# A fused attention, expert and gating kernel: decay factors, tile 0 and tile 1 loaded and scored in another order

## The chip, the core and the metric

The kernel runs on one core of a Trainium2 chip. The metric is the device time of one execution in microseconds (us), as the median of several runs. A profiled execution gives the trace that is read here; it records when each instruction of each engine began and ended, and each transfer. The engines are TensorE (PE in the rows, PEld for its loads of weights), VectorE (DVE), ScalarE (ACT), GpSimd (POOL) and SyncE (SP), which issues most of the transfers.

## What is computed

Three layers follow each other. The first is a linear attention with decay over 2 batches of 8 heads, 768 positions and 64 features, in blocks:

```
intra = einsum('bhic,bhjc->bhij', qb, kb) * Dmask      # Dmask: lam ** (i - j) for j <= i, else 0
intra = einsum('bhij,bhjd->bhid', intra, vb)
inter = einsum('bhid,bhde->bhie', qb * lam_pow, kv_state)
out   = intra + inter
kv_state = lam_block * kv_state + einsum('bhsd,bhse->bhde', kb * rev_pow, vb)
```

The second sends each position to one of 8 experts (the choice of the position before may be kept), which is a product with `w1` (512 x 1024), a maximum with zero and a product with `w2` (1024 x 512), weighted with the softmax of the choice. The third is `(sigmoid(conv(x)) * (x @ w_val)) @ w_out` with a convolution over 5 positions.

## The kernel before

The 1536 positions are cut into 12 tiles `g` of 128, six of each batch. In the first stage, up to about 69 us, each tile runs through the same steps. The later stages (experts one after the other, then convolution and projection) are not touched by the change.

The steps of a tile, by the names of the functions in the code:

- `load_qk(g, part)` (lines 82 to 89) has SyncE load the four quarters of a tile, 256 KB each: quarters 0 and 1 hold queries and keys for the scores (half 0 and half 1), quarter 2 the keys by position, quarter 3 the values. Two quarters with one tile buffer go in one load of 512 KB.
- `scores(g, half)` (line 289): TensorE multiplies keys and queries, 4 matmuls for a half, that is 8 passes, 16 for a tile. The result lies in the banks `ps0` and `ps1`.
- `mask(g)` or `mask_half(g, half)` (lines 301 to 313): VectorE multiplies the scores with the decay mask `dm`.
- `queries(g)` (line 265): VectorE multiplies the queries with the powers `lq`. `powers(hps)` (line 121) makes `lq` by scans on VectorE from the decay factors `lam_sb`; `dm` comes from eight scans of the same factors (line 118).
- `keys(g, hs)` (line 276): ScalarE multiplies the keys of some heads with their decay, one instruction a head. `keys_rest(g)` (line 283): VectorE does the last four heads in one instruction.
- `mix_state(g)`, `mix(g, half)` (lines 315 to 334): TensorE adds the part of the state (not for tile 0) and the part of the masked scores into `po`. `mixed(g)` (line 336): ScalarE copies `po` into `xt`.
- `next_state(g)`, `keep_state(g)`, `decay(g)`: the new state, by TensorE into `sp`, by ScalarE (tile 0) or VectorE out of it, and GpSimd or ScalarE for its decay.
- `turned(g, ks)` (line 380): TensorE turns `xt` back to rows and makes the logits, into the two banks `rt` of the pool `ps_1`, of which there is one buffer. `logits`, `choice`, `shift`, `exponents` and `token_rows` read it on VectorE and ScalarE.

The order of the instructions on each engine is written out by hand: in the block from line 545 on, every engine takes its instructions in the order in which the functions are called. TensorE first runs `warm(8)`, eight matmuls on zeros, then the scores of tile 0, `warm(3)`, the mixing of tile 0, the scores of tile 1, and the rest of tile 0 between the steps of tile 1. From tile 3 on a loop does the same for each tile. The decay factors (6 KB) are loaded by ScalarE's queue at line 67; SyncE's queue begins with the four quarters of tile 0 (lines 105 to 108), each by itself, then two loads of 512 KB for each of the tiles 1 and 2.

Of the kernel before, what the change touches and what calls it, by code (L numbers as in the profile page):

```python
# [8 lines left out]
F32 = mybir.dt.float32  # L9
# [10 lines left out]
B, H, S, D = 2, 8, 768, 64  # L20
DM, E, FF = 512, 8, 1024
P = 128
# [4 lines left out]
HP = H // 2  # L27
# [17 lines left out]
def fused_kernel(ctx, tc, qkv, lam, wgl, w1, w2, wv, cw, wo, out, dbg=None):  # L45
    nc = tc.nc
# [14 lines left out]
    def w4(shape, dtype, name):  # L61
        return w4_p.tile(shape, dtype, name=name, tag="w4")
# [1 line left out]


    lam_sb = const.tile([P, H + HP], F32, name="lam_sb")
    nc.scalar.dma_start(lam_sb, lam)

    ps_ms = ExitStack()
    ps_m = ps_ms.enter_context(tc.tile_pool(name="ps_m", bufs=1, space=PSUM, side="right"))  # L70
# [4 lines left out]
    ps_1 = act.enter_context(tc.tile_pool(name="ps_1", bufs=1, space=PSUM))  # L75
# [6 lines left out]
    def load_qk(g, part=slice(0, 4)):  # L82
        for i in range(2):
            a0, a1 = max(part.start, 2 * i), min(part.stop, 2 * i + 2)
            if a0 < a1:
                if (g, i) not in qk_t:
                    qk_t[g, i] = w4([P, 2, 512], F32, f"qk{i}")
                nc.sync.dma_start(qk_t[g, i][:, a0 - 2 * i:a1 - 2 * i, :],
                                  qkv[g].rearrange("p (a n) -> p a n", a=4)[:, a0:a1, :])
# [12 lines left out]
    identr = const.tile([P, P], F32R, name="identr")  # L102
    wgl_sb = const.tile([P, KD, 9], F32, name="wgl_sb")
    with tc.manual_schedule(engines={mybir.EngineType.SP, mybir.EngineType.DVE}):
        load_qk(0, slice(0, 1))
        load_qk(0, slice(1, 2))
        load_qk(0, slice(3, 4))
        load_qk(0, slice(2, 3))
        load_qk(1, slice(0, 2))
        load_qk(1, slice(2, 4))  # L110
        load_qk(2, slice(0, 2))
        load_qk(2, slice(2, 4))
        nc.vector.memset(ones, 1.0)
        nc.vector.tensor_copy(ident16, ident)
        nc.vector.tensor_copy(identr, ident)

        for h in (0, 1, HP, HP + 1, 2, 3, HP + 2, HP + 3):
            nc.vector.tensor_tensor_scan(dm[:, h, :], lam_sb[:, h:h + 1].to_broadcast([P, P]), last_first, 0.0,
                                         op0=MUL, op1=ADD)

    def powers(hps):

        for hp in hps:
            nc.vector.tensor_tensor_scan(lq[:, hp, :], lam_sb[:, H + hp:H + hp + 1].to_broadcast([P, P]), ones, 1.0,
                                         op0=MUL, op1=MUL)
# [62 lines left out]
    def load_next(n=1):  # L188
        for _ in range(min(n, len(w_src))):
            tiles, src = w_src.pop(0)  # L190
            raw = w4([P, 1024], F32, "wraw")
            nc.sync.dma_start(raw, src)
            tiles.append([raw])
# [65 lines left out]
    sm_t, qs_t, kd_t, xt_t, ps_t, po_t, st_t, sd_t = {}, {}, {}, {}, {}, {}, {}, {}  # L259
# [5 lines left out]
    def queries(g):  # L265
        if g % NC > 0:
            qs_t[g] = qs = at_p.tile([P, HP, P], F32, name="qs", tag="qs")
            nc.vector.tensor_tensor(qs.rearrange("p (a h) i -> p a (h i)", a=2), qk_t[g, 0][:, :, 0:256],
                                    lq.rearrange("p (a h) i -> p a (h i)", a=2), op=MUL)

    def key_tile(g):
        if g not in kd_t:
            kd_t[g] = at_p.tile([P, H, D], F32, name="kd", tag="kd")
        return kd_t[g]

    def keys(g, hs=range(HK)):

        if g % NC < NC - 1:
            kd = key_tile(g)
            for h in hs:  # L280
                nc.scalar.activation(kd[:, h, :], qk_t[g, 1][:, 0, h * D:(h + 1) * D], AF.Copy, scale=dm[:, h, P - 1:P])

    def keys_rest(g):
        if g % NC < NC - 1:
            nc.vector.tensor_tensor(
                key_tile(g)[:, HK:H], qk_t[g, 1][:, 0, HK * D:].rearrange("p (h d) -> p h d", h=H - HK),
                dm[:, HK:H, P - 1:P].to_broadcast([P, H - HK, D]), op=MUL)

    def scores(g, half):
        t = qk_t[g, 0]  # L290

        if half == 0:
            ps_t[g] = [ps_s.tile([P, HP, P], F32, name=f"ps{rh}", tag=f"ps{rh}") for rh in range(2)]
        for hp in (2 * half, 2 * half + 1):
            for rh in range(2):
                r = slice(rh * 64, rh * 64 + 64)
                c0 = (hp % 2) * P
                nc.tensor.matmul(ps_t[g][rh][:, hp, :], t[r, half, 256 + c0:256 + c0 + P], t[r, half, c0:c0 + P],  # L298
                                 start=True, stop=True)
# [7 lines left out]
    def mask_half(g, half):  # L307
        if half == 0:
            sm_t[g] = at_p.tile([P, 2, HP, P], F32, name="sm", tag="sm")
        hs = slice(2 * half, 2 * half + 2)  # L310
        for rh in range(2):
            nc.vector.tensor_tensor(sm_t[g][:, rh, hs], ps_t[g][rh][:, hs],
                                    dm[:, rh * HP + 2 * half:rh * HP + 2 * half + 2, :], op=MUL)

    def mix_state(g):

        po_t[g] = ps_1.tile([P, 2, 512], F32, name="po", tag="po")
        if g % NC > 0:
            qs = qs_t.pop(g)
            for hp in range(HP):  # L320
                for hl in range(2):
                    rh = hl ^ hp % 2
                    r = slice(rh * D, (rh + 1) * D)
                    nc.tensor.matmul(po_t[g][hl * D:(hl + 1) * D, hp % 2, hp // 2 * P:(hp // 2 + 1) * P],  # L324
                                     state[g][r, hp, :], qs[r, hp, :], start=(hp < 2), stop=False)

    def mix(g, half):
        c = g % NC
        for hp in (2 * half, 2 * half + 1):
            for hl in range(2):  # L330
                h = (hl ^ hp % 2) * HP + hp
                nc.tensor.matmul(po_t[g][hl * D:(hl + 1) * D, hp % 2, hp // 2 * P:(hp // 2 + 1) * P],  # L332
                                 qk_t[g, 1][:, 1, h * D:(h + 1) * D], sm_t[g][:, h // HP, hp, :],
                                 start=(c == 0), stop=(c == 0 or hp >= HP - 2))

    def mixed(g):
        xt_t[g] = xt = at_p.tile([P, KD, P], F32, name="xt", tag="xt")
        nc.scalar.copy(xt.rearrange("p (j b) n -> p j b n", b=2),
                       po_t.pop(g)[:, :, 0:2 * P].rearrange("p b (j n) -> p j b n", j=2))
# [12 lines left out]
    def bank(g):  # L352
        if g not in sp_t:
            sp_t[g] = ps_1.tile([P, 512], F32, name="sp", tag="sp")
        return sp_t[g]

    def next_state(g):
        if g % NC < NC - 1:
            st_t[g] = st = bank(g)[:, 0:HP * D].rearrange("p (h d) -> p h d", h=HP)
            kd = kd_t.pop(g)  # L360
            for hp in range(HP):
                for rh in range(2):
                    h = rh * HP + hp
                    nc.tensor.matmul(st[rh * D:(rh + 1) * D, hp, :], kd[:, h, :], qk_t[g, 1][:, 1, h * D:(h + 1) * D],  # L364
                                     start=True, stop=True)
# [14 lines left out]
    def turned(g, ks=range(KD)):  # L380
        if 0 in ks:
            rv_t[g] = ps_1.tile([P, 2, 512], F32, name="rt", tag="rt")
        xt, rt = xt_t[g], rv_t[g]
        for k in ks:
            if k < 2:
                nc.tensor.matmul(rt[:, 0, k * P:k * P + XL], xt[:, k, :], wid[:, k, :], start=(k == 0), stop=False,  # L386
                                 skip_group_check=True)
            else:
                nc.tensor.matmul(rt[:, 0, P:XL], xt[:, k, :], wgl_sb[:, k, :], start=False, stop=(k == KD - 1),  # L389
                                 skip_group_check=True)  # L390
                nc.tensor.transpose(rt[:, 1, (k - 2) * P:(k - 1) * P], xt[:, k, :], ident)  # L391
# [153 lines left out]
    with tc.manual_schedule(engines=order_a):  # L545
# [6 lines left out]
        load_qk(3)  # L552
        load_qk(4)
        load_next()
        powers((0, 1))
        mix_state(0)
        mix(0, 0)
        mix(0, 1)
        mixed(0)
        keys_rest(0)  # L560
        keys(0)
        powers((2, 3))
        scores(1, 0)
        scores(1, 1)
        queries(1)
        turned(0, (0, 1))
        mask_half(1, 0)
        mask_half(1, 1)
        next_state(0)
        keep_state(0)  # L570
        turned(0, (2, 3))
        keys(1)
        keys_rest(1)
        decay(1)
# [380 lines left out]
    early, pt0, yg1 = {}, [], {}  # L955
# [424 lines left out]
def build(nc, arrays):  # L1380
    args = [nc.dram_tensor(f"in_{n}_dram", a.shape, mybir.dt.from_np(a.dtype), kind="ExternalInput").ap()
            for n, a in zip(NAMES, arrays)]
    out = nc.dram_tensor("out_0_dram", (TOK, DM), F32, kind="ExternalOutput").ap()
    with tile.TileContext(nc) as tc:
        fused_kernel(tc, *args, out)
# [11 lines left out]
```

## Time and profile before

| | us |
|---|---|
| median of 3 runs | 320.91 (320.7 to 321.35) |
| the profiled execution | 320.72 |
| its span, first to last instruction | 319.0 |
| TensorE busy in the span | 311.5 (98%) |
| VectorE busy | 260.8 (82%) |
| ScalarE busy | 207.2 (65%) |
| GpSimd busy | 89.8 (28%) |

Times in the rows count from the first instruction of the span. Matmuls are pipelined, so the length of one says less than the distance of a group's beginning to that of the next.

### The profile page before, as it was taken

To read this page: it belongs to the slowest core of one execution; us is meant where nothing else is said; L and a number is where in the kernel's file an instruction comes from. 1 tells how busy PE (TensorE), PEld (TensorE's weight loads), DVE (VectorE), ACT (ScalarE), POOL (GpSimd) and SP (SyncE) were. 2 spreads that over 40 slices of the span, in tenths; PEclk is the share of its full clock that TensorE was granted. 3 is DMA by queue.
4 is the path that set the end of the run, shared out by engine and by line. 5 is a ranking of instruction groups with operands and counts; after the bars stand their busy time and mean duration, and the time that the engine had idled before them with its cause. 6 is when DMAs were issued, how large, how long until landed. Compare 5 with 4: busy or idle time off the path is not lost.

```text
span 319.0 us, 7297 instructions
## 1 busy us (share of the span) xinstructions
PE 311.5 (98%) x2707; PEld 275.9 (86%) x2707; DVE 260.8 (82%) x564; ACT 207.2 (65%) x516; POOL 89.8 (28%) x114
## 2 busy tenths in 40 slices
PE   7999999999999999999999999999999999999995
PEld 3888888889889899899798897988987989989984
DVE  6888899888779979869799797797845899977970
ACT  1679899986557666576567665765656676674641
POOL 8000000204454550542525506433334302020000
PEclk9999999999999999999999999999999999999999
DMA  6999898339779699599598698993305402321112
GB/s 207 403 411 395 301 350 304 125 108 369 258 265 362 247 298 374 204 318 355 158 362 326 184 387 339 325 381 115 107 20 130 132 3 90 109 69 67 65 39 103
DMA packets 27543, 73.09 MB, mean 229 GB/s; under 512 B 3814, under 2 KB 8172, under 8 KB 27500
## 3 DMA queue, kind: packets, MB, share of 16 engines
q1 hardware_dynamic: 24756, 65.07, 56.3%
q0 software_dynamic: 2304, 7.42, 7.2%
q8 instruction: 25, 0.41, 0.5%
q14 instruction: 18, 0.15, 0.1%
q10 hardware_dynamic: 440, 0.05, 0.1%
HBM read 57.79 MB, written 14.73 MB: 227 GB/s over the span
## 4 chain that ended last, share of the span: by engine, by line
PE 93%; DVE 3%; DMA 2%; SPq 1%; ACT 0%; issue 0%; ACTq 0%
PE ph L906 27%; PE py L920 19%; PE pv L1065 11%; PE py L1091 10%; PE py L930 6%; PE ps L298 4%; PE po L332 3%; DMA qk<-in_qkv_dram 2%; PE rt L386 2%; PE po L324 2%; PE sp L364 1%; PE px L879 1%; PE rt L389 1%; PE rt L391 1%; PE pt L1019 1%; PE px L525 1%
## 5 line engine op out<-in xcount | busy, mean ns | idle before, releaser
L203 DVE TENSOR_TENSOR wlo<-wraw,whi 128x1024 fp32r<-128x1024 f32 (+1 forms) x69 | 85.6, 1266 | 12.8 <-ACT whi L198 12.8
L906 PE MATMUL ph<-xh,whi 128*128 128x240 f32 x512 | 87.2, 276 | 0.0
L906 PEld LDWEIGHTS ph<-xh,whi 128*128 128x128 f32 x512 | 77.3, 189 | 2.0 <-issue 1.5
L906 PE MATMUL ph<-xh,wlo 128*128 128x240 f32 x256 | 69.9, 274 | 0.0
L198 ACT CAST whi<-wraw 128x1024 fp32r<-128x1024 f32 (+1 forms) x69 | 65.5, 989 | 2.3 <-DVE wlo L203 2.3
L920 PE MATMUL py<-whi,hh 128*128 128x512 f32 x176 | 56.5, 392 | 0.0
L906 PEld LDWEIGHTS ph<-xh,wlo 128*128 128x128 f32 x256 | 48.4, 189 | 0.0
L1051 DVE SCALAR_TENSOR_TENSOR gt<-yt,cw_sb,gt 128x256 f32<-128x256 f32 x96 | 39.0, 477 | 1.1 <-ACT gt L1043 1.1
L920 PEld LDWEIGHTS py<-whi,hh 128*128 128x128 f32 x176 | 33.0, 188 | 6.7
L909 ACT ACTIVATE hh<-ph 128x480 fp32r<-128x480 f32 x32 | 18.3, 572 | 31.5 <-PE ph L906 29.3
L1065 PEld LDWEIGHTS pv<-yh,wv_t 128*128 128x128 f32 x288 | 35.2, 192 | 0.7 <-ACT gt L1043 0.4
L1065 PE MATMUL pv<-yh,wv_t 128*128 128x256 f32 x288 | 35.7, 283 | 0.0
L227 POOL TENSOR_TENSOR f64a<-f64a,f64s 128x512 f32<-128x512 f32 (+1 forms) x9 | 19.7, 2187 | 55.6 <-DVE f64s L226 55.6
L920 PE MATMUL py<-wlo,hh 128*128 128x512 f32 x88 | 34.4, 391 | 0.0
L1091 PE MATMUL py<-wo_t,gh 128*128 128x512 f32 (+1 forms) x156 | 34.1, 376 | 0.0
L1091 PEld LDWEIGHTS py<-wo_t,gh 128*128 128x128 f32 x156 | 27.4, 188 | 5.0
L911 DVE SCALAR_TENSOR_TENSOR hh<-ph,hh 128x480 fp32r<-128x480 f32 x32 | 20.9, 652 | 6.4 <-ACT hf L910 6.4
L859 POOL DMA_INDIRECT xr<-xd,idx x14 | 19.3, 1378 | 7.2 <-DVE cnt L757 4.2
L920 PEld LDWEIGHTS py<-wlo,hh 128*128 128x128 f32 x88 | 16.5, 188 | 3.2
L930 PE MATMUL py<-wraw,hf 128*64 128x256 f32 x160 | 18.4, 382 | 0.0
L298 PE MATMUL ps<-qk 64*128 64x128 f32 x192 | 16.5, 295 | 0.4 <-DMA qk<-in_qkv_dram 0.4
L930 PEld LDWEIGHTS py<-wraw,hf 128*64 128x64 f32 x160 | 11.0, 137 | 5.5
(201 smaller groups left out, 499.1 us busy)
## 6 DMA issues: line engine op xcount, KB each, us to landing
wraw<-in_w_dram SPq DMA_DIRECT2D x64, 512.0 KB, 6.6
qk<-in_qkv_dram SPq DMA_DIRECT2D x22, 512.0 KB, 7.7
ys<-yo SPq DMA_DIRECT2D x16, 256.0 KB, 4.1
xd<-xtok SPq DMA_DIRECT2D x12, 260.0 KB, 3.9
ys<-warm_sb SPq DMA_DIRECT2D x24, 128.0 KB, 1.9
out_dram<-oo SPq DMA_DIRECT2D x11, 256.0 KB, 2.0
wraw<-in_w_val_dram SPq DMA_DIRECT2D x4, 512.0 KB, 4.0
wraw<-in_w_out_dram SPq DMA_DIRECT2D x4, 512.0 KB, 8.8
```

Of the source, the lines that this page charges most:

```text
L198: nc.scalar.copy(w[1][:, cs], w[0][:, cs])
L203: nc.vector.tensor_tensor(w[2][:, cs], w[0][:, cs], w[1][:, cs].bitcast(F32), op=SUB)
L227: nc.gpsimd.tensor_tensor(a.bitcast(F32), a.bitcast(F32), s.bitcast(F32), op=ADD)
L298: nc.tensor.matmul(ps_t[g][rh][:, hp, :], t[r, half, 256 + c0:256 + c0 + P], t[r, half, c0:c0 + P], start=True, stop=True)
L859: nc.gpsimd.indirect_dma_start(xr[:, t, :], None, xd, bass.IndirectOffsetOnAxis(ap=idx[:, 2 * e + t:2 * e + t + 1], axis=0))
L906: nc.tensor.matmul(ph[:, fi, :], w1_t[e][k][1 + a][:, f * P:(f + 1) * P], xh[b][:, k].rearrange("p t n -> p (t n)")[:, 0:C1], start=first, ...
L911: nc.vector.scalar_tensor_tensor(hh[:, 1, :, 0:C1], ph, 0.0, hh[:, 0, :, 0:C1].bitcast(F32), op0=ALU.max, op1=SUB)
L920: nc.tensor.matmul(py, hhs[f // 2][:, a, f % 2, t * P:(t + 1) * P], w2_t[e][f // 2][1 + b][:, (f % 2) * DM:(f % 2 + 1) * DM], start=(n == ...
L930: nc.tensor.matmul(py[i * NW:(i + 1) * NW, 0:DM // 2], hf[:, f, :], w2_t[e][f // 2][0][:, (f % 2) * DM + i * DM // 2:(f % 2) * DM + (i + 1 ...
L1051: nc.vector.scalar_tensor_tensor(gt[:, k, :], yt_t[b, k][:, c0 + j:c0 + j + 256], cw_sb[:, k, j:j + 1], gt[:, k, :], op0=MUL, op1=ADD)
L1065: nc.tensor.matmul(pv[:, mi, :], wv_t[:, a, k * DM + m * P:k * DM + (m + 1) * P], yh[b][:, k, :], start=first, stop=last)
L1091: nc.tensor.matmul(po, gh[a][:, k, t * P:(t + 1) * P], wo_t[:, b, k * DM + cs.start:k * DM + cs.stop], start=(i == 0), stop=(i == 11))
```

## The change

The decay factors are loaded as the first entry of SyncE's queue, not by ScalarE. Tile 0 comes in two loads of 512 KB (first the quarters for the scores, then keys and values) instead of four of 256 KB. The scores of tile 1 are put ahead of the mixing of tile 0; they use the `rt` banks of `ps_1` instead of `ps0` and `ps1`. All eight heads of tile 0's keys go to ScalarE, ahead of the copy of the mixed tile, and VectorE's instruction for the last four heads of tile 0 is gone. VectorE makes the masks of tile 1 right after those of tile 0, then all powers at once, then the queries of tile 1. TensorE makes the state of tile 0 ahead of the whole of tile 0's turning, which is no longer cut in two.

```diff
-    nc.scalar.dma_start(lam_sb, lam)
...
-        load_qk(0, slice(0, 1))
-        load_qk(0, slice(1, 2))
-        load_qk(0, slice(3, 4))
-        load_qk(0, slice(2, 3))
+        nc.sync.dma_start(lam_sb, lam)
+        load_qk(0, slice(0, 2))
+        load_qk(0, slice(2, 4))
         load_qk(1, slice(0, 2))
         load_qk(1, slice(2, 4))
         load_qk(2, slice(0, 2))
...
-    def scores(g, half):
+    def scores(g, half, early=False):
         t = qk_t[g, 0]
 
-        if half == 0:
+        if half == 0 and early:
+            rt = ps_1.tile([P, 2, HP, P], F32, name="rt", tag="rt")
+            ps_t[g] = [rt[:, rh] for rh in range(2)]
+        elif half == 0:
             ps_t[g] = [ps_s.tile([P, HP, P], F32, name=f"ps{rh}", tag=f"ps{rh}") for rh in range(2)]
...
         load_qk(3)
         load_qk(4)
         load_next()
-        powers((0, 1))
+        scores(1, 0, True)
+        scores(1, 1, True)
+        keys(0, range(H))
         mix_state(0)
         mix(0, 0)
         mix(0, 1)
-        mixed(0)
-        keys_rest(0)
-        keys(0)
-        powers((2, 3))
-        scores(1, 0)
-        scores(1, 1)
-        queries(1)
-        turned(0, (0, 1))
         mask_half(1, 0)
         mask_half(1, 1)
+        mixed(0)
+        powers(range(HP))
         next_state(0)
         keep_state(0)
-        turned(0, (2, 3))
+        queries(1)
+        turned(0)
         keys(1)
         keys_rest(1)
         decay(1)
```

## Rows read from the trace of the kernel before

**Rows 1.** Windows: length, busy time by engine, granted clock, DMA share, GB/s.
```profile
13.00:14.00 1.00, 1.00 (x22) 1.00 (x24) 0.83 (x3) 0.94 (x7) 0.00 (x0) 1.00 1.02 418
...
90.00:240.00 150.00, 150.00 (x1096) 134.61 (x1092) 124.86 (x195) 94.38 (x153) 60.32 (x50) 1.00 0.75 269
```

**Rows 2.** Waits of TensorE's matmuls, the largest after 10 us: total, times, longest.
```profile
PE px L525 <- DVE oh L517: 0.5, 1, 0.5
```

**Rows 3.** Chain of waits from 0 to 14.6 us: start, length, what.
```profile
2.68 6.37 DMA qk<-in_qkv_dram
...
9.18 1.16 PE ps L298 x16
...
11.01 0.62 PE sp L364 x16
...
12.39 0.60 PE po L324 x16
12.99 1.02 PE po L332 x16
```

**Rows 4.** Timeline of TensorE's matmuls, 0 to 9 us: start, length, what.
```profile
1.26 3.23 PE L542 MATMUL pidx<-warm_sb 128*128 128x512 f16 x8 [1.26 <-DVE warm_sb L78]
...
5.57 0.82 PE L542 MATMUL pidx<-warm_sb 128*128 128x512 f16 x3
7.21 1.60 PE L332 MATMUL po<-sm,qk 128*64 128x128 f32 x16 [0.82 <-DVE sm L312]
```

**Rows 5.** Timeline of SyncE: the first and second load issued.
```profile
0.81 0.40 SPq L88 DMA_DIRECT2D qk<-in_qkv_dram  x1
...
1.27 0.42 SPq L88 DMA_DIRECT2D qk<-in_qkv_dram  x1
```

**Rows 6.** Issues of the first, second and fifth load: size, us from issue to landing.
```profile
qk<-in_qkv_dram SPq DMA_DIRECT2D x1, 256.0 KB, 2.9
...
qk<-in_qkv_dram SPq DMA_DIRECT2D x1, 256.0 KB, 3.6
...
qk<-in_qkv_dram SPq DMA_DIRECT2D x1, 512.0 KB, 6.4
```

**Rows 7.** Timeline of SyncE: first and third load of two later bursts.
```profile
157.15 0.39 SPq L192 DMA_DIRECT2D wraw<-in_w_dram  x1
...
158.13 0.38 SPq L192 DMA_DIRECT2D wraw<-in_w_dram  x1
...
198.55 0.39 SPq L192 DMA_DIRECT2D wraw<-in_w_dram  x1
...
199.53 0.38 SPq L192 DMA_DIRECT2D wraw<-in_w_dram  x1
```

**Rows 8.** Issues of these bursts: the first of each, then the third.
```profile
wraw<-in_w_dram SPq DMA_DIRECT2D x1, 512.0 KB, 5.0
...
wraw<-in_w_dram SPq DMA_DIRECT2D x1, 512.0 KB, 7.0
...
wraw<-in_w_dram SPq DMA_DIRECT2D x1, 512.0 KB, 4.2
...
wraw<-in_w_dram SPq DMA_DIRECT2D x1, 512.0 KB, 5.7
```

**Rows 9.** Timeline of VectorE and ScalarE, 3.9 to 10.5 us.
```profile
3.94 2.86 DVE L118 TENSOR_TENSOR_SCAN dm<-lam_sb,last_first 128x128 f32<-128x128 f32 x8 [1.81 <-DMA lam_sb<-in_lam_dram]
...
6.72 1.39 DVE L312 TENSOR_TENSOR sm<-ps,dm 128x256 f32<-128x256 f32 x4
...
8.03 0.72 DVE L124 TENSOR_TENSOR_SCAN lq<-lam_sb,ones 128x128 f32<-128x128 f32 x2
...
8.85 0.59 ACT L338 COPY xt<-po 128x512 f32<-128x512 f32 x1 [5.61 <-PE po L332]
...
9.33 1.06 ACT L281 ACTIVATE kd<-qk,dm 128x64 f32<-128x64 f32 x4
9.75 0.69 DVE L268 TENSOR_TENSOR qs<-qk,lq 128x512 f32<-128x512 f32 x1
```

## The prediction

> **What bounds the kernel now.** I read the busy times of the engines by stretch first, then TensorE's list of waits, then the chain of waits from its beginning, and only then the single loads. Between 90 and 240 us TensorE is busy for all of the 150 us [rows 1]. Its waits after the first ten microseconds are few; the largest that the list shows there is 0.5 us [rows 2]. So from some early point on the kernel is a line of TensorE instructions, and what counts for the end is when that line becomes dense and what still has to run in it from there.
>
> The chain of waits gives the point. It begins with a load: the queries and keys of tile 1 (the first 512 KB load of that tile), issued at 2.68 us, in flight 6.37 us, landed at 9.05. From 9.18 us the chain is TensorE without a hole: scores of tile 1 for 1.16, then the rest of tile 0's work (its state, its turning), and the state part of tile 1's mixing at 12.39 [rows 3]. From 9.18 to 12.39 that is 3.21 us. Before 9.18 TensorE has room: it warms on zeros from 1.26, scores tile 0, warms three times more at 5.57, and mixes tile 0 from 7.21 for 1.60 us, after a wait of 0.82 for VectorE's masks [rows 4]. That mixing is free now, because it lies in the time in which the load of tile 1 is still on its way.
>
> Two things thus decide: when the first load of tile 1 lands, and how much TensorE work stands behind it.
>
> **The change part by part.**
>
> *The mixing of tile 0 goes behind the scores of tile 1.* TensorE takes its instructions in order. With the scores of tile 1 ahead, the 16 passes of tile 0's mixing (and with them its state, its turning and all that follows) are queued behind the wait for that load. What lay in the shadow now lies on the path. Run without holes the same 16 passes take 1.02 us in tile 1 [rows 3]; the 1.60 us of tile 0 hold waits for masks that will be done by then. Cost: +1.02 us.
>
> *The copy of the mixed tile.* Turning tile 0 needs ScalarE's copy of the mixing's result, 0.59 us [rows 9]. Before, the scores of tile 1 covered it. Now only the state matmuls of tile 0 stand between, 0.62 us [rows 3]. With a handover at either end I put the wait at 0.05 us, between 0 and 0.1.
>
> *Powers and queries behind the masks on VectorE.* The state part of tile 1's mixing needs the decayed queries, and VectorE now makes them after four masks (1.39 us) and all four power scans (two take 0.72), in 0.69 [rows 9]. Counted from TensorE's start on the scores of tile 1: half of the scores are done at 0.58, the masks at 0.58 + 1.39 = 1.97, the powers at 1.97 + 1.44 = 3.41, the queries at 4.10. TensorE reaches their reader at 3.21 + 1.02 + 0.05 = 4.28. So there is a margin of 0.18. That a mask starts when its own half is ready is seen in tile 0, where the mixing started at 7.21, when the first of four masks that began at 6.72 had just ended [rows 4, 9]. If it waited for all the scores, the queries would come at 4.7 and TensorE would wait 0.4. I take 0.05; bounds 0 and 0.45. The early scores use the bank of the turning tile, which the masks free at about 2, ahead of the turning at 2.9: nothing.
>
> *All keys of tile 0 on ScalarE.* Four take 1.06 us [rows 9], so eight take 2.1. They stand ahead of the copy of the mixed tile in ScalarE's queue. The keys land as the second load, at about 7 by the bursts below, and the scans that they need as well ended at 6.80 [rows 9], so the keys are done at 9.1 to 9.7; the copy is wanted at about 10.7. Cost nothing while this cover of 1 us lasts; beyond it each microsecond late is one at the end. VectorE is rid of one instruction, which nobody waits for.
>
> *Decay factors first on SyncE's queue.* They are small; only the issue slot counts. The first two loads are issued at 0.81 and 1.27 [rows 5], so each load of the tiles would start 0.46 later. The scans then start where they do now or up to a microsecond earlier, and their readers are no longer near the path: nothing from that side. The Trainium skill ("DMA: Bandwidth & Descriptors", "Issuing engines are not separate DMA queues") says that issuing from another engine saves only the sequencer's time, as all run on the same 16 DMA engines. The row agrees with 0.46 us a slot; by that rule the move buys nothing in bandwidth, and without it the sum below would be 0.46 us lower.
>
> *Two loads of 512 KB for tile 0 instead of four of 256 KB.* Now the first two quarters are both in at 1.27 + 3.6 = 4.87, and the first load of tile 1 at 9.05 [rows 5, 6]. For three loads of 512 KB from an idle queue the trace has bursts of weights. From the first issue to the third landing they take 199.53 + 5.7 - 198.55 = 6.7 and 158.13 + 7.0 - 157.15 = 8.0 us, the quickest and the slowest of four such bursts (the others lie between) [rows 7, 8]. The new loads are exactly such a burst, issued from 1.27: the first load of tile 1 would land between 7.97 and 9.27. The kernel's own start moved its first 512 KB in 4.06 us after the first issue, like the quick burst, whose first load took 4.2, rather than the slow one with 5.0 [rows 8], so I take 7.1: 8.37, which is 0.68 earlier than now.
>
> **Sum.** -0.68 (load) + 1.02 (mixing) + 0.05 (copy) + 0.05 (queries) = +0.44 us. From there on TensorE's line is dense as before, so it reaches the end in full. The profiled execution took 320.72 us (span 319.0 and 1.7 around it) and would take 321.16; it lies 0.19 below the median of the three runs, 320.91, so the median forecast is 321.3.
>
> **The rivals.** A measurement of this kernel tells about 0.2% from no change, 0.64 us.
>
> *Forecast, no difference to be told:* the load lands between 7.97 and 8.55. With 1.12 added and 9.05 taken off that gives 320.9 to 321.5; chance 0.48.
>
> *Slower, the load comes no earlier:* the bursts began with other small traffic out of the way, while here the decay factors and the gate weights are in front, and the first microseconds may be slow whatever the size of a load. The mechanism is one: the third load lands as in the slow bursts. It decides from 8.6 us on; at 9.05 the end moves by 1.12, at 9.27 by 1.34, with the queries' bound of 0.45 instead of 0.05 by 1.7. That is 321.5 to 322.6, in the middle 322.0. For it: two of the four bursts are over 7.5. Against it: the quick start in [rows 6]. Chance 0.34.
>
> *Slower, TensorE's clock falls:* the first load would be in at about 1.27 + 4.06 = 5.3, scores and three warmings end 2.0 later, and TensorE then waits some 1.1 us for the load of tile 1, where its longest wait after the start is now 0.82 [rows 4]. The granted clock is 1.00 in every stretch shown [rows 1], which is the level of 2.4 GHz; the first eight matmuls on zeros, 0.40 us each, ran near the lower level of 1.2 GHz, the last three, after scores, took 0.27 [rows 4]. If the clock fell in the wait and took as long to come back as at the start, 3.23 us of work at the lower level would cost 1.1 to 1.6 us on top: about 322.7. The Trainium skill ("TensorE: Matmul & The Clock Gate", "HAM oscillation — how this bites in real kernels") tells of a kernel that fell back to half clock in each wait for a load; no row here shows a fall after so short a wait, and by that rule the time would be this rival's. Chance 0.06.
>
> *Faster:* the small loads themselves held the queue back. If the first 512 KB came as the first 256 KB did, in 2.9 us [rows 6] plus 0.63 for the other half at the 418 GB/s of the full queue [rows 1], and two more followed at 1.25 each, tile 1 would be there at 1.27 + 3.53 + 2.5 = 7.3: -1.75 + 1.12 = -0.63, so 320.3 or a little less. No burst of the trace is that quick. Chance 0.12, of which a part is for a gain that I don't see.
>
> *The change doesn't do what it says:* the scores of tile 1 can't run before their load, so "ahead of the mixing" buys them nothing, since already now TensorE waits for that load and nothing else at 9.05. This is part of the forecast, not against it.
>
> **How the numbers follow.** Faster 0.12, same 0.48, slower 0.34 + 0.06 = 0.40. The likeliest case gives 321.3. The range leaves out the falling clock and most of the faster case: from 320.4 to 322.3, where the lower end is the quickest burst (320.8) with a share of the faster case and the upper end the slowest burst with some wait for the queries.
>
> **What would show it.** Right: the chain of waits still begins with the first load of tile 1, landed near 8.4; 16 passes of tile 0's mixing stand behind the scores in it; the state part of tile 1's mixing starts 4.2 to 4.4 us after the scores; TensorE has no new wait on VectorE or ScalarE after that. Wrong: a landing near 9 or near 7.3, scores of tile 1 at twice their 1.16 us (clock), a wait of the state part for the queries, or of tile 0's turning for the keys' queue on ScalarE. The forecast fails as a whole if TensorE's line is not dense from there on, so that a shift at the start is swallowed later.

## The result, and the profile after

The median after the change is 322.08 us (321.77 to 324.39, 7 runs), before it 320.71 in the runs taken beside it (320.37 to 321.49, 7 runs): a ratio of 1.0053 by the means of the runs (1.0043 by the two medians), 95% interval 1.0035 to 1.0071. The change makes the kernel slower by 0.35 to 0.71%. The forecast was 321.3, no difference to be told, range 320.4 to 322.3: the time lies in the range, the forecast of no difference is wrong. The profiled execution took 321.96 us with a span of 320.2, against 320.72 and 319.0 before, so the two traces differ by about as much as the medians and the reason must be in them.

The chain of waits of the kernel after, 0 to 16 us (start us, length us, what), is the counterpart of [rows 3]; its last line is from the chain's end, where the last copy of before begins at 315.14:

```profile
2.20 6.52 DMA qk<-in_qkv_dram
...
8.76 1.19 PE rt L299 x16
...
10.31 1.08 DVE sm L313 x3
11.39 1.29 DVE lq L122 x4
...
12.70 0.70 DVE qs L266
13.40 0.14 issue
13.54 0.67 PE po L325 x16
...
316.33 0.37 ACT oo L1100
```

It begins with the same load, now landed at 8.72 instead of 9.05. But after the scores it leaves TensorE. It runs over VectorE: masks of tile 1, all four powers, queries of tile 1. Only at 13.54 does it come back, with the state part of tile 1's mixing. That part began at 12.39 in [rows 3]: +1.15 us (+1.22 by the starts in TensorE's timelines, 12.32 and 13.54). The last copy of the kernel begins 1.19 us later than before, and the span is 1.2 us longer. So the whole difference is made before 13.54 us, and nothing later swallows or adds to it.

The timeline of TensorE's matmuls, after (start us, length us, line, output and inputs, in brackets the idle time before and what ended it), is the counterpart of [rows 4]:

```profile
1.26 3.31 PE L543 MATMUL pidx<-warm_sb 128*128 128x512 f16 x8 [1.26 <-DVE warm_sb L77]
6.22 1.16 PE L299 MATMUL ps<-qk 64*128 64x128 f32 x16 [1.64 <-DMA qk<-in_qkv_dram]
...
8.76 1.16 PE L299 MATMUL rt<-qk 64*128 64x128 f32 x16 [0.62 <-DMA qk<-in_qkv_dram]
9.85 1.09 PE L333 MATMUL po<-sm,qk 128*64 128x128 f32 x16
...
11.68 0.71 PE L387 MATMUL rt<-wid,xt 128*128 128x137 f32 x4 [0.27 <-ACT xt L339]
...
13.54 0.67 PE L325 MATMUL po<-qs,state 64*64 64x128 f32 x16 [0.58 <-DVE qs L266]
```

There are two waits behind the scores of tile 1 that before did not have: 0.27 us for the copy of the mixed tile and 0.58 for the queries. The timeline of VectorE and ScalarE, after, is the counterpart of [rows 9]:

```profile
2.59 3.14 DVE L116 TENSOR_TENSOR_SCAN dm<-lam_sb,last_first 128x128 f32<-128x128 f32 x8 [0.46 <-DMA lam_sb<-in_lam_dram]
7.42 1.42 DVE L313 TENSOR_TENSOR sm<-ps,dm 128x256 f32<-128x256 f32 x4 [1.68 <-PE ps L299]
9.97 1.42 DVE L313 TENSOR_TENSOR sm<-rt,dm 128x256 f32<-128x256 f32 x4 [1.14 <-PE rt L299]
...
7.57 2.02 ACT L279 ACTIVATE kd<-qk,dm 128x64 f32<-128x64 f32 x8 [4.81 <-DMA qk<-in_qkv_dram]
10.99 0.59 ACT L339 COPY xt<-po 128x512 f32<-128x512 f32 x1 [1.41 <-PE po L333]
```

Both groups of masks begin when all 16 passes of their tile's scores are over (7.38 and 9.92), not when the first half is.

### The profile page after: what moved, and what is told of

Same layout as the page of the kernel before. It is cut to its first block, busy times and chain, and to the rows that moved or that the text cites. A ratio compares the mean times of both kernels' runs of the same rounds, so it can differ in the third digit from the quotient of the medians.

```text
span 320.2 us, 7295 instructions
## 1 busy us (share of the span) xinstructions
PE 310.8 (97%) x2707; PEld 275.5 (86%) x2707; DVE 261.3 (82%) x563; ACT 208.7 (65%) x520; POOL 92.4 (29%) x114
## 3 DMA queue, kind: packets, MB, share of 16 engines
HBM read 57.79 MB, written 14.73 MB: 226 GB/s over the span
## 4 chain that ended last, share of the span: by engine, by line
PE 91%; DVE 4%; DMA 2%; ACT 1%; issue 0%; SPq 0%; ACTq 0%
PE ph L904 27%; PE py L918 19%; PE pv L1063 11%; PE py L1089 10%; PE py L928 6%; PE ps L299 4%; PE po L333 3%; DMA qk<-in_qkv_dram 2%; PE rt L387 2%; PE po L325 2%; PE px L877 1%; PE rt L390 1%; PE sp L365 1%; PE rt L392 1%; PE pt L1017 1%; PE px L526 1%
## 5 line engine op out<-in xcount | busy, mean ns | idle before, releaser
L299 PE MATMUL ps<-qk 64*128 64x128 f32 x176 | 15.3, 295 | 1.6 <-DMA qk<-in_qkv_dram 1.6
L1007 POOL DMA_INDIRECT yg<-ys,yslot x6 | 8.3, 1377 | 29.0 <-PE pt L1017 23.1
```

## The experiments

Two explanations stood against each other. One: the order of the work costs the time, that is the mixing put behind the scores, and the masks, powers and queries in one row on VectorE. The other: the new loads cost it, either because they come late or because they leave TensorE idle at the start, so that it reaches its full rate late. The table has all kernels. "Scores" and "state part" are the starts of tile 1's scores and of the state part of its mixing in TensorE's timeline (in the chain of [rows 3] the latter reads 12.39 instead of 12.32, as there the overlap of two groups is taken off), "copy" is the end of the last copy of the kernel; all three are from the one profiled execution of each kernel. Each ratio is to the runs of before taken beside the kernel on the same chip, whose medians were 320.65 to 320.86, and is not the quotient of the two medians; the first row is before as it ran beside after.

| kernel | median us | ratio to before, 95% interval | scores | state part | copy |
|---|---|---|---|---|---|
| before | 320.71 | | 9.18 | 12.32 | 315.51 |
| after | 322.08 | 1.0053, 1.0035 to 1.0071 | 8.76 | 13.54 | 316.70 |
| after, mixing first | 324.36 | 1.0109, 1.0088 to 1.0131 | 11.16 | 15.94 | 319.12 |
| after, powers first | 322.42 | 1.0039, 1.0019 to 1.0059 | 9.41 | 13.54 | 316.65 |
| after, both first | 322.70 | 1.0055, 1.0034 to 1.0075 | 9.36 | 13.34 | 316.57 |
| after, halves apart | 322.73 | 1.0055, 1.0030 to 1.0079 | 9.55 | 14.39 | 317.57 |
| before, both loads' changes | 322.52 | 1.0055, 1.0036 to 1.0075 | 9.77 | 12.90 | 316.11 |
| before, 512 KB loads | 321.44 | 1.0015, 1.0002 to 1.0029 | 9.70 | 12.84 | 316.03 |
| before, factors on SyncE | 321.65 | 1.0018, 1.0002 to 1.0033 | 9.01 | 12.15 | 315.58 |
| after, factors on ScalarE | 321.13 | 1.0007, 0.9989 to 1.0024 | 7.79 | 12.57 | 315.73 |
| after, 12 warmings | 322.15 | 1.0031, 1.0019 to 1.0043 | 8.86 | 13.64 | 316.82 |
| the same, powers first | 321.74 | 1.0025, 1.0014 to 1.0037 | 8.94 | 13.06 | 316.17 |
| before, quarters, then 512 KB | 320.83 | 1.0001, 0.9985 to 1.0017 | 8.74 | 11.88 | 315.05 |
| order alone | 322.02 | 1.0031, 1.0017 to 1.0044 | 9.00 | 14.73 | 317.84 |
| order alone, bridged | 322.44 | 1.0044, 1.0027 to 1.0061 | 8.92 | 13.69 | 317.16 |
| the same, powers first | 321.62 | 1.0034, 1.0021 to 1.0047 | 8.99 | 13.11 | 316.21 |

From the end of the last copy to the end of the span it took 3.4 to 3.7 us in nine of these profiled executions and 4.4 to 4.9 in seven. It was the longer in six of the nine with the decay factors on SyncE's queue (not in after) and in one of the seven with them on ScalarE's; whether that is chance, no run settles. So single times scatter by about 1.2 us for a reason that lies behind all the work looked at here and stays open, and a step is judged by "state part" and "copy". These scatter less: the first load of tile 1 landed at 8.72, 8.82 and 8.90 in three kernels with the same loads (after, 12 warmings, the same with powers first).

**The order undone.** The mixing of tile 0 goes ahead of the early scores again:

```diff
+        mix_state(0)
+        mix(0, 0)
+        mix(0, 1)
         scores(1, 0, True)
         scores(1, 1, True)
         keys(0, range(H))
-        mix_state(0)
-        mix(0, 0)
-        mix(0, 1)
```

> The changed kernel with one thing undone: tile 0's mixing stands ahead of tile 1's scores on TensorE again. Theory A, the 16 passes queued behind the load are what is lost: 1.0 us less than the changed kernel, about 321.1. Theory B, VectorE's row of masks, powers and queries of tile 1 sets when the state part of tile 1's mixing starts, and the mixing lies in its shadow: no gain, since that row still starts when tile 1's scores are done, now after the mixing at about 10.15; state part at 13.5 to 13.8 us from the start against 13.54, 322.0 to 322.3.

It became the slowest of all, 324.36, which neither theory had. The timeline of TensorE:

```profile
6.29 2.08 PE L299 MATMUL ps<-qk 64*128 64x128 f32 x16 [1.43 <-DMA qk<-in_qkv_dram]
8.30 1.46 PE L543 MATMUL pidx<-warm_sb 128*128 128x512 f16 x3
9.69 1.54 PE L333 MATMUL po<-sm,qk 128*64 128x128 f32 x16
11.16 1.16 PE L299 MATMUL rt<-qk 64*128 64x128 f32 x16
```

The scores of tile 0 took 2.08 us where they take 1.16 in the timeline of after, and the three warmings 1.46 instead of 0.82: TensorE still ran at the slow rate of its start, after a hole (idle time) of 1.43 us. (The column of the granted clock reads 1.00 in these stretches, as it does over the first eight warmings at 0.40 us each [rows 4], but that is for want of a record: the trace's record of the clock begins, at 1.00, only at 10.65 us in this run and at 4.16 in after. Until then the rate is seen in the lengths.) The mixing is no longer hidden either: tile 0's first load comes at 6.24 us, and behind it scores, warming and mixing run until 11.2, long past the 8.72 at which the load of tile 1 is there in after. So undoing the order does not bring the old time back while the new loads stand, and a second thing, a late full rate, came in. That the order costs nothing doesn't follow.

**The powers first.** `powers(range(HP))` goes to right behind the masks of tile 0, so that only masks and queries of tile 1 stand behind the scores on VectorE:

```diff
         mask_half(0, 1)
+        powers(range(HP))
...
         mixed(0)
-        powers(range(HP))
```

> The changed kernel with one thing moved: all four power scans stand ahead of tile 1's masks on VectorE, in its idle time after tile 0's masks. Both theories take away the 0.58 us for which TensorE waits for the queries: state part of tile 1's mixing at about 12.95 instead of 13.54, time 0.5 to 0.6 us less than the changed kernel, about 321.5. If the loss lay elsewhere (the loads, the clock), no difference.

The wait for the queries is gone. From the chain of waits:

```profile
10.57 1.05 PE po L333 x16
...
11.64 0.59 ACT xt L339
...
13.61 0.60 PE po L325 x16
```

The chain stays with TensorE and ScalarE's copy, and the state part follows the turning at once, 4.13 us after the scores by the timeline (9.41 to 13.54) instead of 4.78. The median did not fall. In the profiled execution the scores of tile 0 again took 2.08 us and all came 0.65 later; whether that is so in the other eleven runs, one profile doesn't show. This mends one wait and leaves the question of the rate.

**Both.**

> Both moved: mixing of tile 0 ahead of the scores of tile 1, and the powers ahead of tile 1's masks. Theory A: the gains add, 1.0 + 0.6 = 1.6 us less than the changed kernel, 320.5. Theory B: with VectorE's row shortened by the powers, mixing first pays in part: state part at about 12.4, 1.1 us less than the changed kernel, 321.0, which is the time of the kernel before with the load a little earlier.

At the full rate (scores of tile 0 in 1.16) the mixing ran from 7.96 to 9.43 and the scores of tile 1 from 9.36, later than in after. Then the timeline shows a new wait:

```profile
10.57 1.42 DVE L313 TENSOR_TENSOR sm<-rt,dm 128x256 f32<-128x256 f32 x4 [0.57 <-PE rt L299]
...
12.13 0.71 PE L387 MATMUL rt<-wid,xt 128*128 128x137 f32 x4 [1.00 <-ACT kd L279]
```

The turning waited 1.00 us. The row names ScalarE's keys, but `xt` had been copied at 9.46 + 0.59 = 10.05; what ended just before 12.13 are the masks, at 10.57 + 1.42 = 11.99. The early scores occupy the turning's only buffer until the masks have read them. With the mixing behind the scores that is covered (turning at 11.68, masks over at 11.39 in after), as the prediction said; without it, it is not. Neither theory's time came (320.5 or 321.0).

**The halves apart.** The second half of the early scores gets a tile, and so banks, of its own:

```diff
+        elif early:
+            ps_t[g] = [ps_s.tile([P, HP, P], F32, name=f"ps{rh}", tag=f"ps{rh}") for rh in range(2)]
...
```

> The changed kernel with the two halves of tile 1's scores in separate PSUM tiles (half 0 in the banks of the turning tile, half 1 in those of the scores), nothing else moved. If the masks waited for all scores because both halves lie in one tile, the first mask now starts about 0.6 us after the scores' start instead of 1.2, the queries come 0.5 us earlier and the time falls by 0.4 to 0.6 us, to about 321.6. If the masks wait for all scores for another reason, nothing changes: first mask 1.2 us after the scores' start, 322.1.

The timeline of TensorE and VectorE:

```profile
9.55 1.23 PE L301 MATMUL rt<-qk 64*128 64x128 f32 x8
10.57 0.67 PE L301 MATMUL ps<-qk 64*128 64x128 f32 x8
...
10.83 0.76 DVE L315 TENSOR_TENSOR sm<-rt,dm 128x256 f32<-128x256 f32 x2 [1.15 <-PE rt L301]
11.50 0.75 DVE L315 TENSOR_TENSOR sm<-ps,dm 128x256 f32<-128x256 f32 x2
```

The first mask began at 10.83, right behind its own half (over at 10.78) and before the other half ended (11.24). So it is the shared tile that makes it wait for all 16 passes. Whether the program's wait on the tile or the bank itself sets this, the run doesn't separate, as both were parted. The state part still followed the queries: these were over at 14.25, it started at 14.39, 1.40 behind the turning instead of 1.21 with the powers first (12.33 to 13.54). So 0.19 of the wait was left, in a profile whose clock rose in the middle of these scores (its record begins at 10.69). The time shows no gain, and the scores of tile 0 ran at the slow rate again, in 2.08 us.

**The loads alone**, in the kernel before: factors first on SyncE and two loads of 512 KB; then each of the two by itself.

```diff
-    nc.scalar.dma_start(lam_sb, lam)
...
+        nc.sync.dma_start(lam_sb, lam)
+        load_qk(0, slice(0, 2))
+        load_qk(0, slice(2, 4))
```

> The kernel before with the new loads alone: decay factors first on SyncE, tile 0 in two loads of 512 KB; order of the engines as before. If the loads only bring tile 1 earlier (8.7 instead of 9.05): 320.5 to 320.9, state part of tile 1 at about 12.2 to 12.6 us. Theory C: tile 0's scores start at 6.1 instead of 4.4, behind a hole on TensorE, so the clock comes late in part of the executions, and the time is 321.5 to 323.

> The kernel before with tile 0 in two loads of 512 KB and nothing else; the decay factors stay on ScalarE's queue. If the larger first load is what brings tile 0 late, its scores start at 5.3 to 6.1 us (6.1 to 6.5 with both parts of the new loads, 5.0 with the moved factors alone) and the mixing of tile 0, no longer done when tile 1 lands, pushes tile 1's scores to 9.2 or later: 320.8 to 321.6. If the factors' place is the cause, scores start at 4.4 to 5.0 and the time is that of the kernel before or 0.3 less.

> The kernel before with the decay factors alone moved to the head of SyncE's queue, tile 0 still in four loads of 256 KB. If the issue slot is all that it costs, tile 0's first quarter lands 0.46 later (4.2), scores still start on the heels of the warming, tile 1 lands 0 to 0.46 later: 320.8 to 321.3. If small transfers at the head slow the queue's start, the first quarter lands at 5 or later and the time goes to 321.5 or more.

Together they cost 0.58 us at the state part with the old order. TensorE's timeline of that kernel:

```profile
6.52 1.16 PE L296 MATMUL ps<-qk 64*128 64x128 f32 x16 [1.66 <-DMA qk<-in_qkv_dram]
...
8.37 1.47 PE L330 MATMUL po<-sm,qk 128*64 128x128 f32 x16
9.77 1.16 PE L296 MATMUL ps<-qk 64*128 64x128 f32 x16
```

Tile 0 comes so late (6.48) that its mixing no longer fits ahead of tile 1's load: it ran until 9.84, and the scores of tile 1 waited for it, not for their load. The time lies in the range that was expected of a late clock, but the profile shows the full rate. The interval of its times begins at 1.15 us, above the 0.58 of the trace; its profiled execution has the longer end (4.7 us), and if the other five had it too, that would be the rest, but no run shows it. The 512 KB loads with the factors left on ScalarE cost nearly the same, 0.52, by another way:

```profile
0.82 4.28 DMA lam_sb<-in_lam_dram
...
8.12 1.64 PE po L330 x15
9.77 1.09 PE ps L296 x16
```

The chain begins with the 6 KB of decay factors, which land 4.28 us after their issue, beside the big loads, instead of 3.1 before; the scans of the decay mask begin at 5.12 instead of 3.94 [rows 9] and hold up the mixing, while tile 1's load is in at 7.53. The factors first on SyncE, with the quarters kept, lose nothing in the trace up to there (state part 0.17 earlier); its times lie 0.02 to 0.33% above before all the same, and why stays open.

**The change with the factors left on ScalarE.**

```diff
+    nc.scalar.dma_start(lam_sb, lam)
...
-        nc.sync.dma_start(lam_sb, lam)
```

> The changed kernel with the decay factors back on ScalarE's queue. If the factors' slot on SyncE delays every load by 0.46, tile 0 lands at about 5.5 and tile 1 at about 8.3: 0.4 us less than the changed kernel, and fewer late clocks. If the loads' size sets the landing, no difference: tile 0 at 6, tile 1 at 8.7, 322.1 to 322.4.

1.0007, not to be told from before. The first load of tile 1, issued at 1.73 and 5.8 us in flight, lands at 7.53, 1.19 earlier than in after, though the factors' issue slot on SyncE is only 0.46. The scores of tile 1 start 0.97 earlier, as TensorE is busy until then and waits for nothing:

```profile
7.79 1.16 PE L299 MATMUL rt<-qk 64*128 64x128 f32 x16
```

The chain of waits:

```profile
0.82 4.30 DMA lam_sb<-in_lam_dram
...
5.14 0.80 DVE dm L116 x3
...
7.78 1.27 DVE sm L313 x4
...
10.42 1.29 DVE lq L122 x4
...
11.73 0.70 DVE qs L266
```

Now the chain runs over VectorE from 5.14 to the queries: the factors, late again, set the pace. Of the 0.97 us nothing is lost (state part 13.54 to 12.57), but it does no more than pay for the order.

**The hole at the start bridged**, by twelve warmings instead of eight; then also with the powers first.

```diff
-        warm(8)
+        warm(12)
```

> The changed kernel with twelve warming matmuls at the start instead of eight, so that TensorE is busy until tile 0's first load is in at about 6.1 us. Theory C, the hole of 1.5 us behind the warming lets the clock come to 2.4 GHz late in part of the executions: scores of tile 0 in 1.16 us and not in 2.08, state part of tile 1's mixing at about 13.5, which is the changed kernel without its late executions, 321.6 to 322.0 in the median. If the scatter has another cause (loads, the last write), no difference: 322.1 to 322.4, and scores of 2.08 us may still be seen.

> The same twelve warming matmuls, and all four power scans ahead of tile 1's masks on VectorE. With the clock up early, VectorE's row no longer sets the state part of tile 1's mixing: it starts at about 12.95 (13.54 in the changed kernel), 321.3. What then is left against the kernel before is the mixing behind the scores, 1.02 us less the earlier load of 0.3 to 0.4. If the powers don't count, as with the first of these two.

The warmings now last almost until the load is there (a hole of 0.26), the scores of tile 0 run at the full rate, and the median is 322.15, that of after. So a late full rate isn't what the median of after pays for, whose own profile, at 321.96, had the full rate; it may be what makes its slowest runs (324.39), but that is only argued. With the powers first as well, the state part starts 0.58 earlier (13.64 to 13.06), and 321.74 is the lowest of the kernels with all of the change's loads and order. The chain has no VectorE in it:

```profile
8.94 1.16 PE rt L299 x16
10.10 1.05 PE po L333 x16
...
13.13 0.60 PE po L325 x16
```

**The order alone**, with the loads of before; then with ten warmings between the scores of tile 0 and of tile 1 instead of three, and then with the powers first.

```diff
+    nc.scalar.dma_start(lam_sb, lam)
...
-        nc.sync.dma_start(lam_sb, lam)
-        load_qk(0, slice(0, 2))
-        load_qk(0, slice(2, 4))
+        load_qk(0, slice(0, 1))
+        load_qk(0, slice(1, 2))
+        load_qk(0, slice(3, 4))
+        load_qk(0, slice(2, 3))
```

> The changed kernel with the loads of the kernel before: the new order of the engines alone. Tile 1 lands at 9.05 as before, the mixing of tile 0 and VectorE's row of masks, powers and queries stand behind it: state part of tile 1's mixing at 9.18 + 4.78 = 13.96 instead of 12.32, 322.3 to 322.5. If the mixing alone counted, 13.4 and 321.8. No late clock in either case, since tile 0's first quarter lands at 3.7.

In the profiled execution (322.96, the longest of its runs) the rival of the falling clock came true. Its windows (stretch, length, busy time by engine, granted clock, DMA share, GB/s):

```profile
8.00:9.00 1.00, 0.00 (x0) 0.00 (x0) 0.10 (x1) 0.66 (x3) 0.00 (x0) 1.00 1.09 332
9.00:11.00 2.00, 2.00 (x18) 1.77 (x20) 0.00 (x0) 0.00 (x0) 0.00 (x0) 0.54 0.98 350
11.00:13.00 2.00, 2.00 (x30) 2.00 (x32) 1.99 (x7) 0.16 (x1) 0.00 (x0) 0.60 1.04 424
```

and TensorE's timeline:

```profile
9.00 1.96 PE L301 MATMUL rt<-qk 64*128 64x128 f32 x16 [1.85 <-DMA qk<-in_qkv_dram]
```

TensorE, with no mixing to do in the wait for tile 1, stood for 1.85 us; the granted clock was then 0.54 and 0.60 in the mean of two microseconds each (0.50, the level of 1.2 GHz, from 9.17 to 12.59), and the scores took 1.96 us instead of 1.16. To see the order without that, the wait was filled:

```diff
-        warm(3)
+        warm(10)
```

> The new order of the engines with the loads of the kernel before, and ten warming matmuls instead of three between the scores of tile 0 and those of tile 1, so that TensorE does not idle for 1.9 us there. Theory C, idling lets the granted clock fall: it stays 1.00, scores of tile 1 take 1.16 us and not 1.96, and what is left is the order's own price, state part of tile 1's mixing at 9.2 + 4.8 = 14.0 (14.73 with the fall), time 0 to 0.7 us less than without the bridge. If the clock falls in spite of the work on zeros, or the fall was rare, no difference: 322.0.

> The same with all four power scans ahead of tile 1's masks. With the clock held, this takes away the wait for the queries and leaves the mixing behind the scores alone: state part at 13.35 to 13.5 instead of 14.0, 0.5 to 0.6 us less, and against the kernel before the 1.02 us of the mixing and little else, 321.7 to 321.9. If VectorE is late anyway because its masks of tile 0 end at 8.1, the scans come in the way of tile 1's masks and the gain is under 0.3.

Bridged, the granted clock is 1.00 and the scores take 1.16. TensorE's timelines, first bridged, with the queries behind the powers:

```profile
8.92 1.16 PE L301 MATMUL rt<-qk 64*128 64x128 f32 x16
...
13.69 0.67 PE L327 MATMUL po<-qs,state 64*64 64x128 f32 x16 [0.58 <-DVE qs L268]
```

then with the powers first:

```profile
8.99 1.16 PE L301 MATMUL rt<-qk 64*128 64x128 f32 x16
10.08 1.09 PE L335 MATMUL po<-sm,qk 128*64 128x128 f32 x16
11.00 0.63 PE L367 MATMUL sp<-qk,kd 128*64 128x64 f32 x16
11.90 0.71 PE L389 MATMUL rt<-wid,xt 128*128 128x137 f32 x4 [0.27 <-ACT xt L341]
...
13.11 0.67 PE L327 MATMUL po<-qs,state 64*64 64x128 f32 x16
```

The order alone costs 13.69 - 12.32 = 1.37 us, though its scores start 0.26 earlier than before, and 0.58 of it is the row masks, powers, queries. The medians go the same way (322.44 and 321.62), though their intervals overlap; the split rests on the traces, one execution each. The bridge made the median no shorter (322.44, and 322.02 without it on another chip), so nothing shows that the fallen clock is in the median of the order alone.

**A cheaper load.** In the kernel before, only quarters 2 and 3 of tile 0 in one load:

```diff
-        load_qk(0, slice(3, 4))
-        load_qk(0, slice(2, 3))
+        load_qk(0, slice(2, 4))
```

> The kernel before with tile 0's queries and keys still in two loads of 256 KB and only its last two quarters in one of 512 KB. The first scores start at 4.4 as before, on the heels of the warming, and the queue has one load less ahead of tile 1, which lands at 8.5 to 9.0: the same as before or up to 0.4 us less, 320.4 to 320.8. If 512 KB loads at the start only harm, 321.

The scores of tile 1 came 0.44 earlier and the last copy 0.46, but the times are those of before, 1.0001. No kernel here beats before by more than can be told.

## Why the prediction was wrong

From the scores of tile 1 to the state part it is 3.14 us before by TensorE's timeline (9.18 to 12.32; the prediction's 3.21 is the chain's), 4.12 with the new order and no wait for the queries (8.99 to 13.11, order alone, bridged, powers first), and 4.78 after. With a start that is 0.42 earlier (9.18 to 8.76) this is -0.42 + 0.98 + 0.66 = 1.22 us, from 12.32 to 13.54. The prediction had -0.68, 1.07 and 0.05, together 0.44. By its steps:

- *A shift at the start reaches the end in full:* right. State part +1.22, last copy +1.19, span +1.2.
- *Mixing of tile 0 behind the scores, +1.02, and the wait for the copy, +0.05 (0 to 0.1):* the mechanism right, the sizes off both ways. In order alone, bridged, powers first, the 16 passes take 0.92 from their start to that of the next group (10.08 to 11.00); the state with the wait for the copy takes 0.90 (11.00 to 11.90) where it took 0.62 [rows 3], so the copy costs 0.28; and the turning, now in one piece, takes 1.21 (11.90 to 13.11) instead of 1.43 in two [rows 3]. That makes the 0.98.
- *Queries, +0.05 with a bound of 0.45:* the step that failed. It cost 0.66; of the 0.78 that the sum lacked (1.22 - 0.44), 0.61 is here. Its rule was that a mask starts when its own half is ready, read from [rows 4, 9], where the mixing starts after the first of four masks. But that is another handover: TensorE reading finished masks, not VectorE reading scores that TensorE still writes. And in [rows 9] the masks begin at 6.72 when the scans end, so they were held up by VectorE's own row, and the row could not show for what they'd have waited otherwise. In the code each half of the scores writes into both of a tile's banks (the loop over `rh` in `scores`), so no bank is finished at half time. After the change the masks start 1.21 us after the scores, not 0.58; the queries are over 4.64 after, near the 4.7 that the prediction worked out for this case, and the handover to TensorE costs 0.14 more ("issue" before 13.54); TensorE would have been there at 4.12, not 4.28. The profile counts 0.58 of the 0.66 as a wait, above the bound of 0.45. The powers moved away, the wait is gone in three kernels; the halves parted, the first mask starts with its half. The Trainium skill ("PSUM — Partial Sum Buffer", "Terms") says that two engines at once on the same bank and quadrant (32 of the partitions) are an error, TensorE writing and VectorE reading among them. The traces are in keeping with it: in shared banks the masks begin after all passes (9.97, passes over at 9.92), in parted ones before their end (10.83 and 11.24). No run shows the error itself.
- *First load of tile 1 at 8.37:* mis-sized. It landed at 8.72, 0.35 later and within the bounds of 7.97 to 9.27. The burst takes 7.45 us from its first issue, between the two of [rows 7, 8], and not like the quick one. With the factors on ScalarE's queue it takes 6.7 (0.81 to 7.53), like the quick one: what slows it comes with the factors at its head. The sign was right.
- *Decay factors, "only the issue slot counts":* wrong, both ways. With 512 KB loads the factors at the head delay the landing of tile 1's first load by 1.19 (in the order of before by 1.5, from 7.53 to 9.0), not by the slot of 0.46. And the factors' readers are near the path: left on ScalarE's queue beside 512 KB loads they land 1.2 us later, and VectorE's row of scans, masks, powers and queries sets the pace.
- *Keys of tile 0 on ScalarE, nothing:* right. Done at 7.57 + 2.02 = 9.59, the copy began at 10.99.
- *Early scores in the turning's banks, nothing:* right in this order, 1.0 us in another.
- *Rivals:* "load no earlier" was to decide from 8.6 us on and give 321.5 to 322.6. It came half true: 8.72 for a forecast's 1.12 gives +0.79, the rest is the queries. So the time lies in the stated range with a load from the middle of it and a wait beyond its bound: that the upper end was wide enough is in part luck. The clock did not fall in the profile of after, but in one of the order alone, after 1.85 us of idle. "Faster" had no part.

Order alone (bridged) 1.37 and loads alone 0.58 make 1.95, together they make 1.22: in both single changes the mixing of tile 0 lies on the path, and together it is paid once.

## What to carry to other kernels

Work that runs in the wait for a load is free only there; moved behind the load's reader it costs its full length, however early the reader then starts. Before an instruction is said to start on a part of a matmul's result, look whether TensorE still writes the same tile or bank, and whether the row of before shows that wait at all or one on the reader's own engine. And count the row of the engine that serves the first TensorE instruction behind the move, from its first input to its last output, the small load at its head among it.

## What the runs showed of the hardware

A small transfer depends on the large ones beside it. The 6 KB of decay factors took 3.1 us from issue to landing from ScalarE's queue beside loads of 256 KB (before), 4.3 beside loads of 512 KB (both kernels that have this), and 1.8 at the head of SyncE's queue (before with both loads' changes). But there they also keep the large loads back, tile 1's first by 1.19 us. The share of busy DMA engines in 40 slices of 0 to 9 us, first of after, then of after with the factors on ScalarE:

```profile
DMA  0000000046349982187899989998989899899999
```

```profile
DMA  0000000043848898979999999999989999999999
```

With the small load first there are slices at 1 and 2 tenths near 3.5 us, in which nearly nothing moves; without it there are none.

The prediction gave a fall of the clock in a wait of some 1.1 us a chance of 0.06. In the one profile where it fell before the kernel's end, TensorE had stood for 1.85 us, and the granted clock was 0.50 from 9.17 to 12.59 (order alone). At the start it is less plain. Where a hole of 1.2 to 1.4 us followed right after the first eight warmings, the scores of tile 0, from 6.1 us on, still ran near half rate in three profiles (2.08 us), but at the full rate in others with holes of 1.25 to 1.66. The record of the granted clock begins, at 1.00, at 9.28 to 10.69 us in the three, and at 4.16 to 5.13 in the others. Without a hole it begins between 3.99 (before) and 7.12 (the change with the factors on ScalarE, where the scores of tile 0 took 2.08 from 4.98 on, the warmings behind them 0.86). What decides when it comes up late is not settled.
